# RWKV-5 attention and a multiplicative FFN: the products A on 64x64 array tiles, from a copy of the turned k

## The chip, the core and the metric

The kernel runs on one core of one Trainium2 chip. A core has five engines that run their own instruction queues side by side: TensorE (PE, with its weight loads shown apart as PEld), VectorE (DVE), ScalarE (ACT), GpSimd (POOL) and SyncE (SP), which here only issues DMAs. They hand work to one another by semaphores. The metric is the time of one execution on the device in microseconds (us); lower is better.

## The reference, cut to what matters

```
# r, k, v: (4, 8, 768, 48) = batch, head, token, head_dim;  w, u: (8, 48)
for t in range(S):
    kt, vt, rt = k[:, :, t], v[:, :, t], r[:, :, t]
    cur = einsum('bhd,bhe->bhde', u[None] * kt, vt)
    y[:, :, t] = einsum('bhd,bhde->bhe', rt, state + cur)
    state = w[None, :, :, None] * state + einsum('bhd,bhe->bhde', kt, vt)

x = y.transpose(0, 2, 1, 3).reshape(3072, 384)
h = (x @ w1) * (x @ w2) @ w3          # w1, w2: (384, 1024), w3: (1024, 1024)
out = h @ w_out                        # (1024, 384), fp32
```

All of it is fp32 for the tolerance. The four FFN weights arrive as float64 and are read as pairs of 32-bit words.

## The kernel before, in words

**Units.** The 768 tokens of a batch are cut into six chunks of 128. A unit is one chunk of one batch: 24 units, n = 4c + b. A chunk has two halves of 64 tokens. The state `st[b]` is carried from half to half.

**What attention does for one unit.** `scale` (L308, VectorE) multiplies k and r by powers of w, so that inside a half the decay between two tokens comes out as a product of one factor of k and one of r. Then k and r are needed with the head dimension on the partitions ("turned"). For the first five units `turn` does it with TensorE transposes and ScalarE copies (L339, L341). From unit 5 on (`free = B + 1`) `turn_blocks` transposes 32x32 blocks on VectorE (L349) and writes them to a scratch tensor in DRAM (L351), and `turn_places` reads them back with four DMAs into the tile `tts[n % 2]` (L360), where the rows stand with 32 tokens together: `[128, 4 token blocks, 8, 32]`. The first four of the eight are k of the four head pairs, the last four are r.

`pairs(n)` then makes on TensorE the 64-token sums of k times v (`up`, L382) and the products A = k times r inside each half (L389). Both go to one PSUM tile, `ps_a`. As lhsT the old code takes k in slices of 32 tokens, since a contiguous slice of `tts` has only 32, so each of 4 head pairs x 4 token blocks x 2 heads is one product: 32 products on 64x32 tiles of the array. VectorE adds `up` to the state (L402, L403), ScalarE copies the state to the padded tiles `wide` (L414, in `spread`), and VectorE puts A under a mask into the tile `AT` (L410). `AT` has been filled beforehand with the diagonal, from u*k*r, by eight ScalarE instructions (L324, in `diagonal`).

`output(n)` makes y on TensorE from `wide` and the turned r (L467), then from `v` and `AT` (L477); ScalarE copies the result to `xT` (L482).

**The FFN beside it.** For a chunk of all four batches (512 tokens) `ab` makes both first products (L494 and L499); ScalarE copies the first out of PSUM (L496), VectorE multiplies the second by it (L500). w3 and w_out are folded into one matrix first (`fold`, L294 to L299). The last product is done by Strassen's seven products (L533, L539 to L547). The PSUM pool `psF` that these share has two buffers.

**The order.** The loop over units in each visit writes, in source order: loads for later units, `diagonal(n+1)`, `scale` and `turn_blocks(n+2)`, a share of FFN steps, `output(n)`, `turn_places(n+2)`, `pairs(n+1)`, and another share of FFN steps. The tile framework then orders each engine's queue itself, by source order among what it takes to be ready, and inserts the waits. So the queue of an engine isn't the source order: `diagonal` of a later unit, for one, goes to ScalarE as soon as one of the two `AT` buffers comes free.

fp32 products go through the array in two passes, so the profile shows two weight loads and two matmuls for each product: 24 units x 32 products x 2 = 1536 for L389.

Buffers that matter here: `vnat` (v with 48 columns of zeros behind each head) has `NV = 4` of them, `krin` 3, `tts` 2, `AT` 2.

Of the kernel before, what the change touches and what calls it, by code (L numbers as in the profile page):

```python
# [8 lines left out]
F32 = mybir.dt.float32  # L9
# [12 lines left out]
def kernel(  # L22
# [34 lines left out]
    nc = tc.nc  # L57
    B, H, S, D = r.shape
    P = 128
    C = 128  # L60
    T = C // 2
# [3 lines left out]
    NP = H // 2  # L65
# [10 lines left out]
    Q = 32  # L76
# [4 lines left out]
    def rows(i):  # L81
        return slice(i * PAD, (i + 1) * PAD)
# [13 lines left out]
        nc.gpsimd.tensor_copy(out=same[rows(a)], in_=ident[rows(a), rows(a)])  # L96


    NIN, NV, NS, NRAW = 3, 4, 2, 3
    krin = [const.tile([C, 2, H, D], F32, name=f"krin{i}") for i in range(NIN)]  # L100
    vnat = [const.tile([C, H, PD], F32, name=f"vnat{i}") for i in range(NV)]
    krs = [const.tile([C, 2, H, PAD], F32, name=f"krs{i}") for i in range(NS)]
    tts = [const.tile([P, C // Q, 2 * NP, Q], F32, name=f"tt{i}") for i in range(2)]
# [15 lines left out]
        nc.gpsimd.memset(t[:, :, :, D:PAD], 0.0)  # L119
    for t in wide[1] + wide[0]:  # L120
        nc.gpsimd.memset(t, 0.0)


    units = [(c, b) for c in range(NCH) for b in range(B)]
# [2 lines left out]
    def load(n, which="krv"):  # L127
        if n >= NU:
            return
        c, b = units[n]  # L130
        ts = slice(c * C, (c + 1) * C)
        for nm, src, dst in (("k", k, krin[n % NIN][:, 0]), ("r", r, krin[n % NIN][:, 1]), ("v", v, vnat[n % NV][:, :, :D])):
            if nm in which:
                nc.sync.dma_start(out=dst, in_=src[b, :, ts, :].rearrange("h t d -> t h d"))
# [25 lines left out]
    for i in range(2):  # L160
# [4 lines left out]
                      in_=u.rearrange("h d -> (h d)").rearrange("(o n) -> o n", o=1).to_broadcast([P, DM]))  # L165
# [15 lines left out]
    with tc.tile_pool(name="once", bufs=1) as once, tc.tile_pool(name="psW", bufs=2, space=PSUM) as psW:  # L181
# [12 lines left out]
        for l in range(LEVELS):  # L194
            n = 1 << l
# [6 lines left out]
        for g in range(2):  # L202
            nc.vector.tensor_copy(out=both[:, g, :, T:], in_=both[:, g, :, :T])
            ps = psW.tile([P, NP, C], F32, tag="w", name=f"ps_p{g}")
# [7 lines left out]
    def program(fast):  # L212
        with ExitStack() as arm:
            body(arm, fast)

    def body(arm, fast):
        tab = arm.enter_context(tc.tile_pool(name="tab", bufs=1))
        work = arm.enter_context(tc.tile_pool(name="work", bufs=2))
# [11 lines left out]
        else:  # L230
# [6 lines left out]
            for l in range(LEVELS):  # L237
                n = 1 << l
# [7 lines left out]
            ps = psT.tile([P, NP, C], F32, tag="t", name="ps_pr")  # L246
# [55 lines left out]
        kT, rT, AT, xT = {}, {}, {}, {}  # L302
# [9 lines left out]
        def diagonal(n):  # L312

            kr = krin[n % NIN]
            ruk = work.tile([C, H, D], F32, tag="ruk", bufs=1, name=f"ruk{n}")
            dg = work.tile([C, H], F32, tag="dg", bufs=2, name=f"dg{n}")
            nc.vector.tensor_mul(ruk, kr[:, 0], kr[:, 1])
            nc.vector.tensor_mul(ruk, ruk, ub)
            nc.vector.tensor_reduce(dg, ruk, AX.X, ALU.add)
            AT[n] = work.tile([C, 2, NP, T], F32, tag="AT", bufs=2, name=f"AT{n}")  # L320
            for p in range(NP):
                for i in range(2):
                    h = 2 * p + i
                    nc.scalar.activation(out=AT[n][:, i, p, :], in_=same, func=COPY, scale=dg[:, h:h + 1])  # L324


        def turned(n):
            if fast:
                kT[n], rT[n] = (tts[n % 2][:, :, g * NP:(g + 1) * NP].rearrange("x z p t -> x p z t") for g in range(2))
            else:  # L330
                tt = tts[n % 2].rearrange("x z e t -> x (z e t)").rearrange("x (e t) -> x e t", t=C)
                kT[n], rT[n] = (tt[:, g * NP:(g + 1) * NP] for g in range(2))

        def turn(n):
            turned(n)
            for g, dst, nm in ((0, kT, "kT"), (1, rT, "rT")):
                ps = psT.tile([P, NP, C], F32, tag="t", name=f"ps_{nm}{n}")
                for p in range(NP):
                    nc.tensor.transpose(ps[:, p, :], krs[n % NS][:, g, 2 * p:2 * p + 2, :].rearrange("t h d -> t (h d)"),  # L339
                                        ident)  # L340
                nc.scalar.copy(out=dst[n], in_=ps.rearrange("x p (z t) -> x p z t", t=Q) if fast else ps)  # L341

# [6 lines left out]
            nc.sync.dma_start(out=scratch[n].rearrange("z f m e -> (z f) (m e)"), in_=tr.rearrange("x m e t -> x (m e t)"))  # L351

        def turn_places(n):
            turned(n)
            for i in range(2):
                for m in range(3):
                    lo, hi = (max(i * D, m * Q), min((i + 1) * D, (m + 1) * Q))
                    if lo < hi:
                        x = i * PAD + lo - i * D
                        nc.sync.dma_start(out=tts[n % 2][x:x + hi - lo].rearrange("f z e t -> f z (e t)"),  # L360
                                          in_=scratch[n][:, lo - m * Q:hi - m * Q, m, :].rearrange("z f e -> f z e"))

        def pairs(n):

            c, b = units[n]
            kk = krs[n % NS][:, 0]
            if fast:
                au = psA.tile([C, 2, 512], F32, tag="a", name=f"ps_a{n}")
                ps = au[:, :, :NP * T].rearrange("s i (p t) -> s i p t", p=NP)
            else:  # L370
                for l in range(LEVELS):
                    level(n, l)
                kk = work.tile([C, H, PAD], F32, tag="rl", bufs=1, name=f"kk{n}")
                nc.gpsimd.tensor_mul(kk, krs[n % NS][:, 0], pn[:, 0])
                au = psA.tile([C, 2, 512], F32, tag="a", name=f"ps_u{n}")

            up = au[:, :, NP * T:NP * (T + D)].rearrange("x a (p e) -> x a p e", p=NP)
            last = c == NCH - 1
            for p in range(NP):
                for i in range(2):  # L380
                    for a in range(1 if last else 2):
                        nc.tensor.matmul(up[rows(i), a, p, :], lhsT=kk[rows(a), 2 * p + i, :],  # L382
                                         rhs=vnat[n % NV][rows(a), 2 * p + i, 0:D], start=True, stop=True)
            if fast:
                for p in range(NP):
                    for z in range(C // Q):
                        for i in range(2):
                            a = z * Q // T
                            nc.tensor.matmul(ps[z * Q:(z + 1) * Q, i, p, :], lhsT=kT[n][rows(i), p, z],  # L389
                                             rhs=rT[n][rows(i), p, 2 * a:2 * a + 2], start=True, stop=True)  # L390
            by = wc.to_broadcast([P, NP, D])
            if c:
                spread(0, n)
            for a in range(1 if last else 2):
                if not c and not a:
                    if fast:
                        nc.vector.tensor_mul(st[b], up[:, a], by)
                    else:
                        nc.vector.tensor_copy(out=st[b], in_=up[:, a])
                elif fast:  # L400

                    nc.vector.tensor_add(st[b], up[:, a], st[b])  # L402
                    nc.vector.tensor_mul(st[b], st[b], by)  # L403
                else:
                    nc.vector.tensor_mul(st[b], st[b], by)
                    nc.vector.tensor_add(st[b], up[:, a], st[b])
                if not a:
                    spread(1, n)
            if fast:
                nc.vector.copy_predicated(AT[n], later.bitcast(I32)[:, None, None, :].to_broadcast([C, 2, NP, T]), ps)  # L410

        def spread(a, n):
            for i in range(2):
                nc.scalar.copy(out=wide[a][n % 2][rows(i), :, i * D:(i + 1) * D], in_=st[units[n][1]][rows(i)])  # L414
# [179 lines left out]
        free = B + 1 if fast else NU + 1  # L594
        scale(0)
        diagonal(0)
        turn(0)
        pairs(0)
        asked = 2
        for c in range(NCH):  # L600
            plan = beside[c]
            if not isinstance(plan[0], list):
                cuts = [len(plan) * m // (2 * B) for m in range(2 * B + 1)]
                plan = [plan[cuts[m]:cuts[m + 1]] for m in range(2 * B)]
            for b in range(B):
                n = c * B + b
                while asked <= (n + 3 if n + 3 >= free else n + 2):
                    load(asked)
                    asked += 1
                if n + 1 < min(NU, free):  # L610
                    scale(n + 1)
                if n + 1 < NU:
                    diagonal(n + 1)
                if n + 1 < min(NU, free):
                    turn(n + 1)
                if free <= n + 2 < NU:
                    scale(n + 2)
                    turn_blocks(n + 2)
                for step in plan[2 * b]:
                    step()  # L620
                output(n)
                if free <= n + 2 < NU:
                    turn_places(n + 2)
                if n + 1 < NU:
                    pairs(n + 1)
                for step in plan[2 * b + 1]:
                    step()
# [41 lines left out]
```

## Time and profile before

| | |
|---|---|
| median of 3 runs | 539.51 us (538.28 to 539.96) |
| profiled execution, span | 536.4 us |
| TensorE busy | 502.8 us, 94% |
| VectorE / ScalarE busy | 282.2 us (53%) / 184.1 us (34%) |
| DMA packets, share of 16 engines | 35.1% |
| A products (L389): matmul busy, instructions | 23.3 us, 1536 |
| granted TensorE clock, mean | 0.987 |

The time is that of the whole execution; the profile's span is from the first to the last instruction of the program. A group's line gives the busy time, the mean of one instruction, and after the bar the idle time of its engine just before such instructions with what ended it. "issue" is idle time for which the profile shows no wait. Matmuls overlap, so the busy time of a group of small ones is much less than count times mean.

### The profile page before, as it was taken

The numbers are of one execution on the slowest core, as the hardware profiler recorded it, in microseconds if no ns is written. First come the engines' busy times: TensorE is split into PE (matmuls) and PEld (weight loads), VectorE is DVE, ScalarE is ACT, GpSimd is POOL, SyncE is SP. The second block draws the span as 40 slices with busy tenths as digits, with TensorE's granted clock in tenths as the row PEclk, the third lists the DMA queues.
The fourth block names the chain that finished last, engine by engine and source line by source line (L and its number), as shares of the span: only waits on it lengthen the run. The fifth ranks groups of instructions, "written<-read, shape, count | busy, mean of one in ns | idle before, by whom it ended". The sixth has DMA issues, their size and how long they took to land.

```text
span 536.4 us, 13739 instructions
## 1 busy us (share of the span) xinstructions
PE 502.8 (94%) x5960; PEld 329.6 (61%) x5960; DVE 282.2 (53%) x616; ACT 184.1 (34%) x468; POOL 5.5 (1%) x22
## 2 busy tenths in 40 slices
PE   2777999998999999999999999999999999999997
PEld 2656555544555566559645974487554777954486
DVE  5789897578764664493642464324531215311342
ACT  3787475466553565430123023113033110000100
POOL 4000000000000000000000000000000000000000
PEclk9788999999999999999999999999999999999999
DMA  7978655757665463340131313202011000000001
GB/s 186 226 179 259 202 133 151 204 165 185 177 181 147 135 194 107 76 104 31 45 90 30 104 55 97 60 27 78 31 60 32 2 31 30 31 29 1 0 0 66
DMA packets 96871, 52.82 MB, mean 98 GB/s; under 512 B 77729, under 2 KB 88226, under 8 KB 96802
## 3 DMA queue, kind: packets, MB, share of 16 engines
q1 hardware_dynamic: 96802, 51.86, 35.1%
q8 instruction: 49, 0.80, 0.6%
q14 instruction: 20, 0.16, 0.1%
HBM read 39.65 MB, written 12.19 MB: 97 GB/s over the span
## 4 chain that ended last, share of the span: by engine, by line
PE 86%; ACT 5%; DVE 4%; issue 2%; DMA 2%; SPq 0%; DVEq 0%; ACTq 0%
PE ps_a L494 23%; PE ps_b L499 22%; PE ps_w L298 8%; PE ps_y L467 4%; PE ps_y L477 4%; PE ps_a12b L533 3%; PE ps_s3t L533 3%; PE ps_s4b L533 3%; PE ps_s1t L533 3%; PE ps_a22t L533 3%; PE ps_s2t L533 3%; PE ps_a11b L533 3%; PE ps_a L389 3%; ACT AT L324 2%; PE ps_a L382 1%
## 5 line engine op out<-in xcount | busy, mean ns | idle before, releaser
L494 PE MATMUL ps_a<-xT,w 128*128 128x512 f32 (+1 forms) x300 | 134.2, 582 | 4.2 <-issue 1.8
L499 PE MATMUL ps_b<-xT,w 128*128 128x512 f32 (+1 forms) x300 | 132.5, 577 | 0.2 <-DVE abt L500 0.2
L499 PEld LDWEIGHTS ps_b<-xT,w 128*128 128x128 f32 x300 | 56.6, 190 | 66.1 <-issue 61.2
L500 DVE TENSOR_TENSOR abt<-ps_b,a 128x512 f32<-128x512 f32 (+1 forms) x50 | 33.4, 669 | 115.4 <-PE ps_b L499 110.3
L494 PEld LDWEIGHTS ps_a<-xT,w 128*128 128x128 f32 x300 | 55.1, 190 | 62.9 <-issue 55.8
L496 ACT COPY a<-ps_a 128x512 f32<-128x512 f32 (+1 forms) x50 | 28.4, 567 | 162.9 <-PE ps_a L494 152.6
L324 ACT ACTIVATE AT<-same,dg 128x64 f32<-128x64 f32 x192 | 48.5, 336 | 0.3
L414 ACT COPY wide<-st 64x192 f32<-64x192 f32 x88 | 30.7, 349 | 44.5 <-PE ps_y L467 27.7
L298 PE MATMUL ps_w<-wo,w3T 128*128 128x384 f32 x128 | 43.1, 490 | 1.7 <-ACT w3T L295 1.7
L308 DVE TENSOR_TENSOR krs<-krin,pn_in 128x768 f32<-128x768 f32 x24 | 22.9, 956 | 21.5 <-PE ps_a L382 15.3
L298 PEld LDWEIGHTS ps_w<-wo,w3T 128*128 128x128 f32 x128 | 23.7, 190 | 17.2 <-ACT w3T L295 2.1
L467 PEld LDWEIGHTS ps_y<-tt,wide 128*32 128x32 f32 x1056 | 18.7, 113 | 24.1 <-issue 13.9
L467 PE MATMUL ps_y<-tt,wide 128*32 128x64 f32 x1056 | 26.0, 228 | 5.5 <-ACT wide L414 3.8
L269 ACT ACTIVATE t<-raw,two 128x512 f32<-128x512 uint32 (+2 forms) x32 | 25.3, 799 | 16.8 <-DVE w3n L267 8.0
L389 PE MATMUL ps_a<-tt 64*32 64x64 f32 x1536 | 23.3, 231 | 4.5 <-issue 4.5
L264 ACT ACTIVATE power<-raw 128x512 f32<-128x512 f32 (+2 forms) x32 | 22.3, 703 | 14.6 <-DMA raw<-in_moe_w_dram 11.1
L265 DVE TENSOR_SCALAR power<-power 128x512 f32<-128x512 f32 (+2 forms) x32 | 14.0, 438 | 23.4 <-ACT power L264 23.4
L477 PE MATMUL ps_y<-AT,vnat 64*64 64x64 f32 x1152 | 23.6, 230 | 0.4 <-DVE AT L410 0.4
L539 ACT COPY m<-ps_a11b 128x192 f32<-128x192 f32 x12 | 3.8, 318 | 57.7 <-PE ps_a11b L533 57.7
L477 PEld LDWEIGHTS ps_y<-AT,vnat 64*64 64x64 f32 x1152 | 20.2, 141 | 4.2 <-DVE st L403 1.5
L389 PEld LDWEIGHTS ps_a<-tt 64*32 64x32 f32 x1536 | 18.5, 109 | 6.7 <-issue 5.3
L349 DVE STREAM_TRANSPOSE tr<-krs 128x768 f32<-128x768 f32 x19 | 18.5, 976 | 0.5
(90 smaller groups left out, 566.5 us busy)
## 6 DMA issues: line engine op xcount, KB each, us to landing
raw<-in_moe_w_dram SPq DMA_DIRECT2D x16, 512.0 KB, 4.7
scratch<-tr SPq DMA_DIRECT2D x19, 384.0 KB, 3.2
raw<-in_moe_w_dram SPq DMA_DIRECT2D x8, 768.0 KB, 5.6
tt<-scratch SPq DMA_DIRECT2D x38, 128.0 KB, 2.7
krin<-in_k_dram SPq DMA_DIRECT2D x24, 192.0 KB, 3.8
krin<-in_r_dram SPq DMA_DIRECT2D x24, 192.0 KB, 4.2
vnat<-in_v_dram SPq DMA_DIRECT2D x24, 192.0 KB, 3.7
out_dram<-osb SPq DMA_DIRECT2D x24, 192.0 KB, 1.9
```

The source lines that it names most:

```text
L269: nc.scalar.activation(out=t, in_=lo, func=IDENTITY, bias=two, scale=2.0 ** -51)
L298: nc.tensor.matmul(ps, lhsT=w3T[:, kc, :], rhs=wo[kc], start=(kc == 0), stop=(kc == KF - 1))
L324: nc.scalar.activation(out=AT[n][:, i, p, :], in_=same, func=COPY, scale=dg[:, h:h + 1])
L389: nc.tensor.matmul(ps[z * Q:(z + 1) * Q, i, p, :], lhsT=kT[n][rows(i), p, z], rhs=rT[n][rows(i), p, 2 * a:2 * a + 2], start=True, stop=True)
L414: nc.scalar.copy(out=wide[a][n % 2][rows(i), :, i * D:(i + 1) * D], in_=st[units[n][1]][rows(i)])
L467: nc.tensor.matmul(to(a, q, g), lhsT=wide[a][n % 2][:, p, j * Q:(j + 1) * Q], rhs=rw[:, p, 2 * a:2 * a + 2] if fast else rw[:, p, rows(a)] ...
L477: nc.tensor.matmul(ps[rows(g), a, q, :], lhsT=vv[rows(a), x:x + PAD], rhs=AT[n][rows(a), h % 2, h // 2, :], start=(a not in held and (a, g ...
L494: nc.tensor.matmul(pa[:, :n], lhsT=w1[:, z, q, js], rhs=xT[c][:, q, ts], start=(q == 0), stop=(q == KM - 1))
L496: nc.scalar.copy(out=a[:, :n], in_=pa[:, :n])
L499: nc.tensor.matmul(pb[:, :n], lhsT=w2[:, z, q, js], rhs=xT[c][:, q, ts], start=(q == 0), stop=(q == KM - 1))
L500: nc.vector.tensor_mul(abt[c, j][:, ts], pb[:, :n], a[:, :n])
L533: nc.tensor.matmul(ps, lhsT=made[c, j][a][:, m * C:(m + 1) * C], rhs=made[b][:, j, :], start=(j == 0), stop=(j == KH - 1))
```

## The change

Three things are done.

1. The turned k is given a tile of its own, `kT`, `[128, 4 pairs, 128 tokens]`, one buffer, in which the 128 tokens of a pair stand together. For the first five units `turn` writes it straight from PSUM. From unit 5 on the new `turn_rows(n + 1)` copies it out of `tts` on ScalarE, right behind `diagonal(n + 1)` in the source: 19 copies of 128x512.
2. With 64 tokens together, A is made from 4 pairs x 2 halves x 2 heads = 16 products with a 64x64 lhsT and a 64x64 tile of the array in place of 32 with 64x32. The sums are the same.
3. To make room in SBUF, `vnat` goes from four buffers to three, and v is loaded for unit n + 2 where it was for n + 3. The k half of `tts` is cleared once at the start on GpSimd, since `turn` no longer writes it.

```diff
-    NIN, NV, NS, NRAW = 3, 4, 2, 3
+    NIN, NV, NS, NRAW = 3, 3, 2, 3
...
+    for t in tts:
+        nc.gpsimd.memset(t[:, :, :NP], 0.0)
...
         def turned(n):
+            kT[n] = work.tile([P, NP, C], F32, tag="kT", bufs=1, name=f"kT{n}")
             if fast:
-                kT[n], rT[n] = (tts[n % 2][:, :, g * NP:(g + 1) * NP].rearrange("x z p t -> x p z t") for g in range(2))
+                rT[n] = tts[n % 2][:, :, NP:].rearrange("x z p t -> x p z t")
...
-                nc.scalar.copy(out=dst[n], in_=ps.rearrange("x p (z t) -> x p z t", t=Q) if fast else ps)
+                nc.scalar.copy(out=dst[n], in_=ps.rearrange("x p (z t) -> x p z t", t=Q) if fast and g else ps)
...
+        def turn_rows(n):
+            turned(n)
+            nc.scalar.copy(out=kT[n].rearrange("x p (z t) -> x p z t", t=Q),
+                           in_=tts[n % 2][:, :, :NP].rearrange("x z p t -> x p z t"))
...
                 for p in range(NP):
-                    for z in range(C // Q):
+                    for a in range(2):
                         for i in range(2):
-                            a = z * Q // T
-                            nc.tensor.matmul(ps[z * Q:(z + 1) * Q, i, p, :], lhsT=kT[n][rows(i), p, z],
+                            nc.tensor.matmul(ps[rows(a), i, p, :], lhsT=kT[n][rows(i), p, rows(a)],
                                              rhs=rT[n][rows(i), p, 2 * a:2 * a + 2], start=True, stop=True)
...
-                    load(asked)
+                    load(asked, "kr")
                     asked += 1
+                load(n + 2, "v")
...
                 if n + 1 < NU:
                     diagonal(n + 1)
+                    if n + 1 >= free:
+                        turn_rows(n + 1)
```

More of the change, by code (lines that the diff above doesn't have):

```diff
@@ L327, in turned @@
         def turned(n):
+            kT[n] = work.tile([P, NP, C], F32, tag="kT", bufs=1, name=f"kT{n}")
             if fast:
-                kT[n], rT[n] = (tts[n % 2][:, :, g * NP:(g + 1) * NP].rearrange("x z p t -> x p z t") for g in range(2))
+                rT[n] = tts[n % 2][:, :, NP:].rearrange("x z p t -> x p z t")
             else:
-                tt = tts[n % 2].rearrange("x z e t -> x (z e t)").rearrange("x (e t) -> x e t", t=C)
-                kT[n], rT[n] = (tt[:, g * NP:(g + 1) * NP] for g in range(2))
+                rT[n] = tts[n % 2].rearrange("x z e t -> x (z e t)").rearrange("x (e t) -> x e t", t=C)[:, NP:]
         def turn(n):
@@ L353, in turn_places @@
         def turn_places(n):
-            turned(n)
             for i in range(2):
```

## The prediction, made before the changed kernel was run

> **What bounds the kernel now.** I read the busy table and slices first, then the chain of waits, then the timeline of single visits, because a mean over 24 visits hides which engine sets the pace of each. From the page:
>
> ```profile
> PE   2777999998999999999999999999999999999997
> ACT  3787475466553565430123023113033110000100
> ...
> q8 instruction: 49, 0.80, 0.6%
> ...
> PE 86%; ACT 5%; DVE 4%; issue 2%; DMA 2%; SPq 0%; DVEq 0%; ACTq 0%
> ...
> L477 PE MATMUL ps_y<-AT,vnat 64*64 64x64 f32 x1152 | 23.6, 230 | 0.4 <-DVE AT L410 0.4
> L389 PE MATMUL ps_a<-tt 64*32 64x64 f32 x1536 | 23.3, 231 | 4.5 <-issue 4.5
> ```
>
> From about 60 us on TensorE is the bound: 9 tenths in nearly every slice and 86% of the chain. So time taken out of TensorE's queue counts, unless ScalarE (5% of the chain) is what a visit waits for. The two last lines are the ones to compare: L477 already runs on 64x64 tiles, L389 on 64x32, and L389 has 4.5 us of idle time without a visible wait.
>
> The timeline of an undisturbed visit (weight loads; start and length in us):
>
> ```profile
> 318.91 0.79 PEld L477 LDWEIGHTS ps_y<-AT,vnat 64*64 64x64 f32 x48
> ...
> 319.61 0.56 PEld L382 LDWEIGHTS ps_a<-vnat,krs 64*64 64x64 f32 x32
> ...
> 320.22 0.80 PEld L389 LDWEIGHTS ps_a<-tt 64*32 64x32 f32 x64
> ...
> 321.12 0.30 PEld L494 LDWEIGHTS ps_a<-xT,w 128*128 128x128 f32 x2
> ```
>
> From start to start: 48 passes of L477 take 0.70 us, 14.6 ns each. 32 of L382, on the same tiles, would take 0.47 at this pace, but 0.61 go by before L389: 0.14 are the change of tile size. 64 of L389 with the change to 128x128 behind them take 0.90.
>
> A visit with the idle time in it:
>
> ```profile
> 403.78 0.59 PEld L389 LDWEIGHTS ps_a<-tt 64*32 64x32 f32 x49
> ...
> 405.31 0.18 PEld L389 LDWEIGHTS ps_a<-tt 64*32 64x32 f32 x15 [0.94 <-issue]
> ```
>
> TensorE stops in the middle of independent products. I counted TensorE's instructions through the trace: the five such stops in L389 (112, 267, 292, 334 and 404 us), one of 1.84 us in L494 at 129.7 and one of 0.87 in L467 at 90.3 all stand at place 193 or 194 modulo 256. Queue q8 moved 0.80 MB in 49 packets, 16 KB each: 256 instructions of 64 bytes. So TensorE ran into the end of a block of its own instructions before the next had come.
>
> ScalarE's part, the chain in visit 13 (the visit named by the unit whose A it makes):
>
> ```profile
> 189.95 0.93 PE ps_y L477 x48
> ...
> 190.90 0.48 ACT xT L482
> 191.38 1.92 ACT AT L324 x8
> 193.30 0.48 ACT w3T L295
> ...
> 193.82 2.20 PE ps_w L298 x6
> ```
>
> L389 isn't on it: TensorE is through with it and waits for ScalarE. The chain goes through AT L324 in this way in visits 5, 11, 13 and 14.
>
> **What the Trainium skill says.** The Trainium skill, "TensorEngine Tiling (Array Packing)", Key Properties: a change of tile size drains TensorE, a change of tile doesn't. The trace agrees: the 0.14 us above. "TensorE: Matmul & The Clock Gate", LDWEIGHTS: a weight load's time goes by its columns. L477 and L382 agree in pace at equal columns, though their moving operands have 64 and 48; half as many loads of twice the columns then gain little in loading itself. "Runtime: NRT & Kernel Launch", Instruction fetch mechanics: instructions come in 16 KiB blocks of 256, and crossing a boundary is mostly hidden. The block size agrees; "hidden" doesn't hold in the dense stretches here. "TensorE: Matmul & The Clock Gate", Architectural detail: ScalarE's queue is strictly first in, first out. The trace has ScalarE standing 2.63 us before L264 for a DMA at 189.41, with later work behind it.
>
> **The change, part by part.**
>
> *Products.* 32 passes in place of 64 and one change of tile size less. Before, L382 and L389 took 321.12 - 319.61 = 1.51 us. After: 64 passes of 64x64 at 14.6 ns = 0.93, plus one change at the end, taken as 0.14 to 0.20: 1.07 to 1.13. The gain is 0.4 us a visit. Visit 13 gives the same before, 192.06 - 190.57 = 1.49. Visits in which L389 lies on the chain: 1, 6 to 10, 12, 15 to 23, sixteen. 16 x 0.4 = 6.4 us. In the other eight it lies beside ScalarE, VectorE or a load and is worth nothing. Bounds: 0.3 x 16 = 4.8 and 0.4 x 24 = 9.6.
>
> *Instruction blocks.* A dense stretch (L467, L477, L382, L389) is 384 instructions before and 320 after. TensorE stops if a whole block of 256 lies in it: 128 places out of 256 before, 64 after, plus about 6 for the slower instructions behind. Chances of 0.52 and 0.27 a visit; seven stops of about 1 us before would become about four. Shifting all places by 64 a visit also gives me four, in other visits. That would be 3 us, but where they fall is luck, and one that falls in a visit paced by ScalarE costs nothing either way: I take 2, from -1 to 5.
>
> *The copy.* 19 times 128x512 on ScalarE. Its nearest rows in the tile view and on the page:
>
> ```profile
> L341 ACT COPY tt<-ps_kT x5: 557/561/588, 12.5 to 47.9; 128x512 f32<-128x512 f32 x5
> ```
> ```profile
> L414 ACT COPY wide<-st 64x192 f32<-64x192 f32 x88 | 30.7, 349 | 44.5 <-PE ps_y L467 27.7
> ```
>
> L341 reads PSUM: 0.56 us. L414 goes from SBUF to SBUF as the new copy does, 349 ns for 192 elements; the price in the Trainium skill, "ScalarE: Activation LUTs", What ACT_TABLE_LOAD costs (186 ns and 0.833 ns an element, 346 ns here) agrees, and gives an estimate of 0.61 us for 512. I take 0.6: 11.6 us busy in all, harmless where ScalarE waits for TensorE, as it does for most of the time after 235 us.
>
> Its wait is dearer. It needs the four DMAs of L360, which start only when `output` has read the old `tts`:
>
> ```profile
> 189.98 2.91 SPq L360 DMA_DIRECT2D tt<-scratch  x4
> ```
> ```profile
> DMA to landing us min/median/max: 2.1/3.0/5.7
> ```
>
> In visit 13 the last of the four is issued between 191.3 and 192.9 and lands near 195. If the copy stands in ScalarE's queue right behind AT L324 (free at 193.3), ScalarE stands until 195 and the w3T copies behind it, for which TensorE waits, come 2.4 us late. If the queue is made with the copy behind them, nothing is lost. The same reckoning gives at most 0.6 in visit 5, 1.5 in 7 (the wide copies), 0.5 in 10, 1.1 in 11, 1.6 in 14 and 0.8 in 17 (m L539); elsewhere the next ScalarE work that TensorE needs is a L496, with the 2.6 us of the other product as slack. Sum between 0 and 8.5. The framework puts instructions where it takes them to be ready, so some will stand behind: I take 3.4, two fifths.
>
> *Nothing:* v one unit later goes into the buffer that `output(n - 1)` frees in both versions, and still has about two visits (over 15 us) for a landing of 3.7. kT with one buffer waits for `pairs` of the unit before, which TensorE has always finished by then. The two memsets on GpSimd (5.5 us busy in all) are needed first at unit 5.
>
> Sum: 539.5 - 6.4 - 2 + 3.4 = 534.5 us.
>
> **The rivals.** *More gain:* the copy always stands behind what TensorE needs (0.5 in place of 3.4), and three stops go: 539.5 - 6.4 - 3 + 0.5 = 530.6. For it: ScalarE is 34% busy. Against it: DMAs take 2.1 to 5.7 us, and the queue order is fixed beforehand. *Slower:* ScalarE becomes the bound of a visit; all of the 8.5 us come, and one more stop: 539.5 - 6.4 + 8.5 + 1 = 542.6. For it: in visits 5, 11, 13 and 14 ScalarE is already what TensorE waits for, and ScalarE has waited for DMAs before. Against it: all have to go wrong at once. *No change:* some 6 us of waits against the 6.4, and the stops merely move: 539.5.
>
> **How the numbers follow.** Chances: forecast 0.50, more gain 0.18, no change 0.13, slower 0.19. Below 537.9 (0.3%) are the forecast and the case of more gain: 0.68 faster, 0.13 the same, 0.19 slower. The range reaches from just below the better case to the slower one, 529.5 to 542.5: what is outside is a gain in all 24 visits, or waits of over 8.5 us.
>
> **What would show it.** Right: L389 with 768 matmuls of 64*64; L382's start to the start of what follows L389 near 1.1 us in place of 1.5; fewer than seven stops; a new ScalarE copy of 0.6 us, 19 times, with waits for tt<-scratch of a few us in all. Wrong: L389's passes slower than 14.6 ns, waits for the copy or for w3T and wide behind it of more than 5 us on TensorE, or as many stops as before.

## The result, and the profile after

| | before | after |
|---|---|---|
| median of 4 runs | 539.38 us (538.28 to 539.96) | 525.77 us (524.83 to 526.36) |
| after to before | | 0.9749 [0.9727, 0.977] |
| profiled execution, span | 536.4 us | 522.9 us |
| stops at the end of an instruction block, from visit 5 on | 7, 9.3 us | 2, 1.5 us |
| start of visit 5 | 69.8 us | 66.4 us |

The changed kernel is 13.6 us faster, 2.5%. The forecast was 534.5 and the range began at 529.5, so the gain is 8.7 us larger than forecast. "Visit" is used as in the prediction, and "stop" for TensorE standing still for over 0.5 us at place 193 or 194 modulo 256 of its instruction count. The length of a stop is the time between the starts of the two loads around it, less the 15 ns of a dense stretch. In L494, where the loads stand 0.43 us apart anyway, that is 0.4 us too much: the seven stops of before are 8.9 us without it.

In the code after, a few lines have moved: L382 is now L389, L389 is L395, L467 is L473, L477 is L483, L324 is L326, L295 is L297, L298 is L300, L494 is L500. The new copy of k is L367.

The same parts of the page as were shown of before (slices, instruction queue, chain, the two groups of 64x64 products):

```profile
PE   2697999999999999999999999999999999999996
...
ACT  3897485566655667330223124222243110001000
...
q8 instruction: 43, 0.70, 0.6%
...
PE 85%; DVE 6%; ACT 4%; SPq 2%; issue 2%; DMA 1%; DVEq 0%; ACTq 0%
...
L483 PE MATMUL ps_y<-AT,vnat 64*64 64x64 f32 x1152 | 24.2, 232 | 1.6 <-DVE AT L416 1.6
...
L395 PE MATMUL ps_a<-tt,kT 64*64 64x64 f32 x768 | 18.3, 230 | 0.7 <-issue 0.7
```

TensorE is the bound as before, and ScalarE's share of the chain didn't grow. The A products are 768 on 64x64, and their idle time without a visible wait went from 4.5 to 0.7 us. Six fewer blocks of instructions were fetched (43 in place of 49 packets).

The timeline of visit 18 after (start and length in us, weight loads):

```profile
309.38 0.79 PEld L483 LDWEIGHTS ps_y<-AT,vnat 64*64 64x64 f32 x48
310.08 0.56 PEld L389 LDWEIGHTS ps_a<-vnat,krs 64*64 64x64 f32 x32
310.54 0.58 PEld L395 LDWEIGHTS ps_a<-tt,kT 64*64 64x64 f32 x32
311.20 0.30 PEld L500 LDWEIGHTS ps_a<-xT,w 128*128 128x128 f32 x2
```

From L389 to what follows L395 there are 1.12 us; before, the same stretch of visit 18 took 1.51. L389 takes 0.46 us up to L395, which is 32 passes at 14.6 ns with nothing on top: the change of tile size that cost 0.14 us there is gone. This is what the Trainium skill, "TensorEngine Tiling (Array Packing)", Key Properties, says of a change of tile that keeps the size.

What is left of the stops, in visit 16 after:

```profile
258.54 0.56 PEld L389 LDWEIGHTS ps_a<-vnat,krs 64*64 64x64 f32 x32
259.00 0.54 PEld L395 LDWEIGHTS ps_a<-tt,kT 64*64 64x64 f32 x27
260.39 0.20 PEld L395 LDWEIGHTS ps_a<-tt,kT 64*64 64x64 f32 x5 [0.85 <-issue]
260.66 0.30 PEld L500 LDWEIGHTS ps_a<-xT,w 128*128 128x128 f32 x2
```

TensorE stands for 0.85 us after 27 of 32 independent loads. There is one more in the trace, 0.6 us in L473 at 86.1.

### The profile page after: what moved, and what is told of

The parts are those of the page before. It is cut to its first block, busy times and chain, and to the rows that moved or that the text cites. A ratio compares the mean times of both kernels' runs of the same rounds, so it can differ in the third digit from the quotient of the medians.

```text
span 522.9 us, 12272 instructions
## 1 busy us (share of the span) xinstructions
PE 495.6 (95%) x5192; PEld 324.3 (62%) x5192; DVE 281.8 (54%) x616; ACT 195.7 (37%) x487; POOL 6.0 (1%) x23
## 4 chain that ended last, share of the span: by engine, by line
PE 85%; DVE 6%; ACT 4%; SPq 2%; issue 2%; DMA 1%; DVEq 0%; ACTq 0%
PE ps_b L505 22%; PE ps_a L500 22%; PE ps_w L300 8%; PE ps_y L483 4%; PE ps_y L473 3%; PE ps_s3t L539 3%; PE ps_s4b L539 3%; PE ps_s1t L539 3%; PE ps_a22t L539 3%; PE ps_a12b L539 3%; PE ps_s2t L539 3%; PE ps_a11b L539 3%; PE ps_a L395 2%; PE ps_a L389 1%; ACT AT L326 1%
## 5 line engine op out<-in xcount | busy, mean ns | idle before, releaser
L500 PE MATMUL ps_a<-xT,w 128*128 128x512 f32 (+1 forms) x300 | 134.8, 586 | 0.0
L500 PEld LDWEIGHTS ps_a<-xT,w 128*128 128x128 f32 x300 | 56.1, 192 | 58.4 <-issue 53.0
L326 ACT ACTIVATE AT<-same,dg 128x64 f32<-128x64 f32 x192 | 48.7, 336 | 0.3
L300 PE MATMUL ps_w<-wo,w3T 128*128 128x384 f32 x128 | 43.1, 490 | 2.3 <-ACT w3T L297 2.3
L300 PEld LDWEIGHTS ps_w<-wo,w3T 128*128 128x128 f32 x128 | 23.7, 190 | 17.8 <-ACT w3T L297 2.8
L473 PEld LDWEIGHTS ps_y<-tt,wide 128*32 128x32 f32 x1056 | 18.4, 112 | 23.7 <-issue 15.9
L473 PE MATMUL ps_y<-tt,wide 128*32 128x64 f32 x1056 | 25.3, 226 | 6.3 <-ACT wide L420 3.6
L266 ACT ACTIVATE power<-raw 128x512 f32<-128x512 f32 (+2 forms) x32 | 22.4, 706 | 10.6 <-DMA raw<-in_moe_w_dram 9.7
L483 PE MATMUL ps_y<-AT,vnat 64*64 64x64 f32 x1152 | 24.2, 232 | 1.6 <-DVE AT L416 1.6
L483 PEld LDWEIGHTS ps_y<-AT,vnat 64*64 64x64 f32 x1152 | 20.7, 144 | 6.4 <-DVE AT L416 2.0
L267 DVE TENSOR_SCALAR power<-power 128x512 f32<-128x512 f32 (+2 forms) x32 | 14.0, 439 | 10.8 <-ACT power L266 10.6
L488 ACT COPY xT<-ps_y 128x384 f32<-128x384 f32 x24 | 11.4, 475 | 21.4 <-PE ps_y L483 15.8
L395 PE MATMUL ps_a<-tt,kT 64*64 64x64 f32 x768 | 18.3, 230 | 0.7 <-issue 0.7
```

Source lines behind the costliest of these rows:

```text
L300: nc.tensor.matmul(ps, lhsT=w3T[:, kc, :], rhs=wo[kc], start=(kc == 0), stop=(kc == KF - 1))
L395: nc.tensor.matmul(ps[rows(a), i, p, :], lhsT=kT[n][rows(i), p, rows(a)], rhs=rT[n][rows(i), p, 2 * a:2 * a + 2], start=True, stop=True)
L473: nc.tensor.matmul(to(a, q, g), lhsT=wide[a][n % 2][:, p, j * Q:(j + 1) * Q], rhs=rw[:, p, 2 * a:2 * a + 2] if fast else rw[:, p, rows(a)] ...
L483: nc.tensor.matmul(ps[rows(g), a, q, :], lhsT=vv[rows(a), x:x + PAD], rhs=AT[n][rows(a), h % 2, h // 2, :], start=(a not in held and (a, g ...
L500: nc.tensor.matmul(pa[:, :n], lhsT=w1[:, z, q, js], rhs=xT[c][:, q, ts], start=(q == 0), stop=(q == KM - 1))
```

## The experiments

Two things needed separating: the products (fewer and shorter passes) from the stops, and both from the copy and the later v. The first theory was that the stops follow from the place of each instruction alone, so that any shift of the count changes the time. The rival was that they belong to the 64x32 products, or that the gain comes from the start of the kernel.

**Where the stops fall: shifted copies of both kernels.** Some small products, whose result nobody reads, are put at the head of TensorE's queue. That moves the count of everything behind them and changes nothing else in the queues.

```diff
+        pad = psW.tile([P, T], F32, tag="pad", bufs=1, name="pad")
+        for x in range(26):
+            nc.tensor.matmul(pad[0:Q, :], lhsT=ident[:, 0:Q], rhs=ident[:, 0:T], start=True, stop=True)
```

Four instructions for each: 26 products move the kernel before by 104 places, 44 by 176; 34 and 22 move the changed kernel by 136 and 88.

> The kernel before, with 26 small products ahead of everything (104 more TensorE instructions, done while TensorE waits for its first data). Nothing else in any queue changes; only the ends of the 256-instruction blocks fall elsewhere. Theory (a stop wherever a whole block lies in a dense stretch, less the 32 or so instructions for which the next block is asked ahead): stops leave visits 9, 16, 17, 19 and 22 and come in visits 5, 10, 11, 12, 13, 14, 15, 18 and 23, besides 7; some ten in place of seven, 11 us in place of 7, of which some 2.5 are hidden behind ScalarE in visits 5, 11, 13 and 14: about 541.5 us (540.5 to 543). Rival (the stops belong to certain visits, to DMA traffic or to the 64x32 tiles as such): the same visits as before, 539.4 us.

> The same with 44 small products, 176 instructions. Theory: stops in visits 11, 19, 20 and 21, and a short one in 6; about 5 us in place of 7: 537.5 us (536.5 to 539). Rival: the same visits as before, 539.4 us.

> The changed kernel with 34 small products ahead, 136 instructions. Theory: no stop of over 0.5 us is left; the two of the changed kernel (0.3 and 0.7 us) go: 524.8 us (524.0 to 525.6). Rival: no difference, 525.8 us.

> The changed kernel with 22 small products ahead, 88 instructions. Theory: stops of about 1 us in visits 9, 11 and 17, that of visit 11 partly hidden behind ScalarE: 3 us in place of 1, 527.0 us (526.2 to 528.0). Rival: no difference, 525.8 us.

Measured beside the kernel before (539.64 us): the kernel before shifted by 104, 535.39 us, ratio 0.9918 [0.9894, 0.9942]; by 176, 535.04, 0.9925 [0.9904, 0.9945]. The changed kernel shifted by 136, 524.13, 0.9714 [0.9679, 0.9749]; by 88, 525.92, 0.9751 [0.9715, 0.9786].

So the kernel before gains 0.8% from 104 or 176 instructions that compute nothing. The stops did move. In the kernel before shifted by 104 one now stands in visit 18, which had none:

```profile
314.87 0.61 PEld L481 LDWEIGHTS ps_y<-AT,vnat 64*64 64x64 f32 x35
315.39 0.56 PEld L386 LDWEIGHTS ps_a<-vnat,krs 64*64 64x64 f32 x32
316.01 0.72 PEld L393 LDWEIGHTS ps_a<-tt 64*32 64x32 f32 x59
317.76 0.14 PEld L393 LDWEIGHTS ps_a<-tt 64*32 64x32 f32 x5 [1.03 <-issue]
```

L393 is L389 of before, moved by the added lines. But not every stop that had been foretold came: after the shift by 104 those of visits 5, 11, 15, 18 and 23 did and those of visits 7, 10, 12, 13 and 14 didn't; after the shift by 176 visits 6, 11, 19 and 20 did and 21 didn't, and one came in visit 8 that hadn't been foretold. A block of 256 that lies wholly in a dense stretch isn't enough for a stop. Both shifted kernels before had been expected at a different time, too (541.5 and 537.5), so the rule was incomplete. The changed kernel shifted by 136 came out near the 524.8 of the theory, though one stop of 1.0 us stayed where none had been foretold; shifted by 88 it came out at its rival's 525.8. The count over the traces below mends the rule.

**One part at a time: v alone, and the copy with the old 32 products.** The first has three `vnat` tiles and v loaded for n + 2, nothing else; a twin has the later load with four tiles. The other is the whole change except the products:

```diff
-                    for a in range(2):
+                    for z in range(C // Q):
                         for i in range(2):
-                            nc.tensor.matmul(ps[rows(a), i, p, :], lhsT=kT[n][rows(i), p, rows(a)],
+                            a = z * Q // T
+                            nc.tensor.matmul(ps[z * Q:(z + 1) * Q, i, p, :], lhsT=kT[n][rows(i), p, z * Q:(z + 1) * Q],
```

> The kernel before with the v part alone: three v tiles, v loaded for unit n + 2. Theory (the 3.4 us that the changed kernel is ahead when visit 5 begins come from v standing later in SyncE's queue, so that k, r and the first weights come sooner): 3 us less, 536.4 us (535.4 to 538), unless the stops at block ends fall differently. Rival (those 3.4 us come from the copy kT and the shorter products): 539.4 us.

> The same, v loaded for unit n + 2, but with the four v tiles of before. Theory (the order of the loads does it, not the wait for a free tile): like the v part alone, 536.4 us. Rival (the wait of v for the third tile does it, by holding v back still longer): less or no gain, 538 to 539.4 us.

> The changed kernel, with kT and its copy and the later v, but with the 32 products on 64x32 tiles. Theory (the copy costs nothing, since its place in ScalarE's queue is behind what TensorE needs): the time of the v part alone within 1.5 us, about 536.5. Rival (the copy costs the 3.4 us that I took for it): 539.5 to 540.

Measured, beside 539.4 us before: v alone 536.62, 0.9946 [0.9921, 0.997]; with four tiles 538.55, 1.0003 [0.9985, 1.002]; the copy with 32 products 540.13, 1.0014 [1.0, 1.0029]. The whole gain thus lies in going from 32 to 16 products: without that step, the change is worth nothing.

Two of the three weren't as expected. The later load with four tiles gained nothing, where 536.4 had been expected. The copy with 32 products came out at its rival's number (539.5 to 540, the copy costs what I took for it) and not at 536.5: it is 3.5 us above v alone. In the traces 3.0 of that are stops (9.6 against 6.6 us, last table), but the medians alone would also fit a v that gains 2.8 and a copy that costs 3.5. The copy made twice, below, speaks against that cost.

And the stops of the kernel before are back with the 32 products, this one in visit 17 of the kernel with the copy:

```profile
294.37 0.56 PEld L389 LDWEIGHTS ps_a<-vnat,krs 64*64 64x64 f32 x32
294.99 0.51 PEld L396 LDWEIGHTS ps_a<-tt,kT 64*32 64x32 f32 x43
296.81 0.26 PEld L396 LDWEIGHTS ps_a<-tt,kT 64*32 64x32 f32 x21 [1.31 <-issue]
```

**Is it the 64x32 tile or the number of instructions? Each of the 16 products made twice.** The tile stays 64x64, and TensorE's count of instructions is that of the 32 products.

```diff
-                            nc.tensor.matmul(ps[rows(a), i, p, :], lhsT=kT[n][rows(i), p, rows(a)],
-                                             rhs=rT[n][rows(i), p, 2 * a:2 * a + 2], start=True, stop=True)
+                            for x in range(2):
+                                nc.tensor.matmul(ps[rows(a), i, p, :], lhsT=kT[n][rows(i), p, rows(a)],
+                                                 rhs=rT[n][rows(i), p, 2 * a:2 * a + 2], start=True, stop=True)
```

> The changed kernel with each of the 16 products made twice in a row, which writes the same sums again: as many TensorE instructions as before, on 64x64 tiles. Theory (stops come from the number of instructions that stand closely together): 32 more passes at 14.6 ns in some 15 visits are 7 us, and stops of 4 to 6 us come back: 537.5 us (535.5 to 539.5). Rival (stops came with the small tiles): 532.8 us.

Measured: 547.83 us, 1.0163 [1.0131, 1.0195]. Visits 17 and 20 in its trace:

```profile
301.37 0.43 PEld L396 LDWEIGHTS ps_a<-tt,kT 64*64 64x64 f32 x19
302.64 0.54 PEld L396 LDWEIGHTS ps_a<-tt,kT 64*64 64x64 f32 x21 [0.84 <-issue]
...
370.24 0.56 PEld L389 LDWEIGHTS ps_a<-vnat,krs 64*64 64x64 f32 x16
370.70 1.17 PEld L396 LDWEIGHTS ps_a<-tt,kT 64*64 64x64 f32 x64
371.94 0.30 PEld L501 LDWEIGHTS ps_a<-xT,w 128*128 128x128 f32 x2
```

Visit 17 stops again, now in 64x64 products, and so do 7, 9, 16 and 22: five of the six visits in which the copy with 32 products stops. The stops go with the number of small instructions in a row, not with the tile. The time had been expected 10 us lower; it is 22.1 above the changed kernel. The 64 passes take 371.94 - 370.70 = 1.24 us in place of 0.66 (visit 18 after, 311.20 - 310.54), so 0.58 more in each visit, where 32 passes at 14.6 ns in some 15 visits had been expected. From visit 5 on that is 10.7 us in 19 visits, and 2.7 more of stops (last table). The other 9.1 us come before visit 5; 3.5 of them are one stop in L501 at 38.7 us, and the rest wasn't taken apart. The added passes make a product again on the tile just used. They cost 0.58 / 32 = 18 ns each, where a pass of the changed kernel costs 14.6.

**Fewer stops by choice: shifts picked by the mended rule.** With the rule that the block must begin well inside the dense stretch, 51 added products should leave three stops in the kernel with the copy and 32 products, 50 do much the same for v alone, and 11 take the last stops from the changed kernel. A fourth kernel is that last one with each copy L367 made twice.

> The changed kernel with the 32 products on 64x32 tiles, and 51 small products (204 instructions) ahead, so that by the places seen so far stops remain in visits 9, 16 and 19 alone. Theory (stops are made by where the ends of the blocks fall, nothing else): its stops go from 9.9 us to 3.6: 533.8 us (532.5 to 536). Rival: as without the 204 instructions, 540.1 us.

> The changed kernel with 11 small products (44 instructions) ahead: no stop is left by the places seen so far. Theory: 524.4 us (523.6 to 525.2), the fastest of all. Against the 32 products with three stops (533.8) it is then 9.4 us faster, of which 3.6 are stops and some 6 the products' own passes. Rival: no gain over 525.8 us.

> The v part alone with 50 small products (200 instructions) ahead: stops in the same three visits as with the copy and 204 instructions. Theory (the copy costs nothing): the same time as that run within 1 us, 533.5 us (532 to 535). Rival (the copy costs what the two runs without shift differ by, 3.5 us): 530 us.

> The changed kernel with 44 instructions ahead and each of the 19 copies of the turned k made twice, 11.7 us more work on ScalarE. Theory (ScalarE has room where the copies stand): the time of the run with 44 instructions within 0.6 us, 524.6 us. Rival (the copy is on the path in the visits paced by ScalarE): 2 to 4 us more, 526.5 to 528.5.

Measured, beside 539.86 us before: 539.23, 0.9988 [0.9974, 1.0001]; 525.60, 0.9738 [0.9711, 0.9765]; 538.43, 0.9971 [0.9953, 0.9989]; and with each copy twice 525.43, 0.9735 [0.9711, 0.9758].

With 32 products no shift helped as hoped (533.8 and 533.5 us had been expected): seven and five stops in the whole trace, not three. Some fall where no small product stands any more, just behind the stretch, as in visit 17 of the kernel with the copy, shifted by 204:

```profile
294.83 0.77 PEld L400 LDWEIGHTS ps_a<-tt,kT 64*32 64x32 f32 x64
295.70 0.79 PEld L544 LDWEIGHTS ps_a11b<-w,abt 128*128 128x128 f32 x5
297.34 0.46 PEld L544 LDWEIGHTS ps_a11b<-w,abt 128*128 128x128 f32 x3 [0.86 <-issue]
```

All 64 loads of L400 run through, and TensorE stops some ten instructions behind them, at the block's end. With 16 products the shift by 44 leaves no stop at all; in its page the group of A products has no idle time:

```profile
L399 PE MATMUL ps_a<-tt,kT 64*64 64x64 f32 x768 | 18.8, 237 | 0.0
```

Yet it isn't measurably faster than the changed kernel (524.4 had been expected): 1.5 us of stops are gone, but its visit 5 began at 68.1 us instead of 66.4. That is within what the start of the kernel varies by from trace to trace (last table).

The copy made twice adds 10.6 us of busy time to ScalarE (195.6 to 206.2 in the two pages) and nothing to the time (525.43 against 525.60):

```profile
L372 ACT COPY kT<-tt x38: 601/618/621, 56.7 to 397.3; 128x512 f32<-128x512 f32 x38
```

**All traces side by side.** For each trace: the start of visit 5, the stops from then on, the time from visit 5 to the end, and that time without the stops, in us; the last column is the median of the runs.

| kernel | products | visit 5 begins | stops from then on | visit 5 to the end | without stops | time |
|---|---|---|---|---|---|---|
| before | 32 | 69.8 | 7, 9.3 | 466.6 | 457.3 | 539.4 |
| before, shifted 104 | 32 | 70.3 | 5, 5.8 | 462.4 | 456.6 | 535.4 |
| before, shifted 176 | 32 | 68.6 | 5, 6.2 | 464.5 | 458.2 | 535.0 |
| v alone | 32 | 71.6 | 6, 6.6 | 465.4 | 458.7 | 536.6 |
| v later, four tiles | 32 | 69.7 | 7, 9.3 | 467.0 | 457.6 | 538.6 |
| copy, 32 products | 32 | 71.2 | 6, 9.6 | 467.6 | 458.0 | 540.1 |
| the same, shifted 204 | 32 | 70.8 | 6, 7.0 | 467.3 | 460.3 | 539.2 |
| v alone, shifted 200 | 32 | 69.1 | 4, 6.2 | 468.2 | 462.0 | 538.4 |
| after | 16 | 66.4 | 2, 1.5 | 456.4 | 454.9 | 525.8 |
| after, shifted 44 | 16 | 68.1 | 0 | 454.7 | 454.7 | 525.6 |
| the same, copies twice | 16 | 69.0 | 0 | 454.8 | 454.8 | 525.4 |
| after, shifted 136 | 16 | 66.9 | 1, 1.0 | 454.7 | 453.7 | 524.1 |
| after, shifted 88 | 16 | 67.6 | 2, 2.5 | 456.2 | 453.7 | 525.9 |
| after, products twice | 16, twice | 75.5 | 5, 4.2 | 469.8 | 465.6 | 547.8 |

The 32-product kernels have four to seven stops of 5.8 to 9.6 us together, the 16-product kernels at most two of 2.5, wherever the count is shifted to; with the 16 made twice, five are there again. So it isn't luck that the changed kernel lost them.

## Why the forecast was off, step by step

**What bounds it: right.** TensorE is the bound before and after, and what was taken out of its queue came out of the time.

**Products: 6.4 us forecast, about 6.6 measured, but partly elsewhere.** The gain in a steady visit is as said (1.51 to 1.12 in visit 18, 1.50 to 1.09 in visits 20 and 21). From visit 5 on, without stops, the 16-product kernels take 454.4 us on average (five traces) and the 32-product ones 458.6 (eight), which is 4.2; without the outlier of 462.0 it is 3.7. That is nine or ten visits' worth, where the forecast had fifteen (6.0 us). The rest, 2.9 us, lies before visit 5, where the forecast had one visit (0.4 us). That the two sums agree is luck. There the 32 products with v loaded late reach visit 5 at 70.5 (five traces), the 16 products, with v loaded late too, at 67.6 (five). TensorE's clock is low in that part (0.77 between 14 and 36 us before, 0.84 after), so a pass that is saved there may be a longer one; that wasn't tried by itself.

Visit 13 shows why other visits give nothing. The part of its timeline after that answers to the chain shown of before:

```profile
182.44 0.56 PEld L389 LDWEIGHTS ps_a<-vnat,krs 64*64 64x64 f32 x32
...
183.15 2.02 ACT L326 ACTIVATE AT<-same,dg 128x64 f32<-128x64 f32 x8
...
185.07 1.05 ACT L297 COPY w3T<-ps_w3T 128x512 f32<-128x512 f32 x2
...
185.69 2.23 PEld L300 LDWEIGHTS ps_w<-wo,w3T 128*128 128x128 f32 x8 [0.83 <-ACT w3T L297]
...
188.31 0.61 ACT L367 COPY kT<-tt 128x512 f32<-128x512 f32 x1
```

From L389 to L300 there are 3.25 us, and before they were 193.82 - 190.57 = 3.25 as well. TensorE is through sooner and waits longer for w3T (the weight load 0.83 in place of 0.49 us). Here the saved time comes back as a wait, which isn't a cost of the copy.

**Instruction blocks: the step that failed.** "I take 2, from -1 to 5": 7.8 us were gained (9.3 to 1.5; 7.4 without the ordinary spacing in L494). "Seven stops of about 1 us before would become about four": they became two, and the seven were 1.3 us each. What was right is that the stops are block ends, and that shorter stretches have fewer. What was wrong is the window. I took a stop to come wherever a whole block of 256 lies in the dense stretch, which gives 134 places of 256 before and 70 after. I took ten traces (all but those shifted by 44, 200 and 204) and for each block after 60 us that ends in a dense stretch (or between its groups), with at least 200 of its instructions in it, counted how many dense instructions stand ahead of the block:

```
dense instructions ahead of the block   blocks   stops over 0.5 us
57 or more                              36       36   (0.54 to 1.68 us)
31 to 45                                14        4
0 to 30                                  9        1
none, the stretch begins in the block   45        1
```

The four traces left out, whose shifts were picked by this, give 6 of 6, 0 of 4 and 1 of 9 for the first three rows. So, as a rule, TensorE must also have come some 45 places into the dense stretch before the block begins, or the next block is there in time.

The packets of q8, whose times the traces keep, show why. Counted in order, one packet falls to each block, and by the times of the stops it brings the next one. In visit 9 of before, the block that ends in the stop begins at 110.71 us. The packet starts at 111.37 and has landed at 112.59, and TensorE goes on at 113.83. The window from 111.3 to 112.7 has this packet (one, of 0.02 MB), and that from 112.65 to 113.83 has none:

```profile
q8 instruction: 1, 0.02, 5.5%
```

All 62 stops of the fourteen traces end 1.14 to 1.60 us after such a packet has landed. Of the 78 blocks after 60 us that lie wholly in a dense stretch, 48 end in a stop: their packet starts 0.40 to 1.47 us after the block itself does. For the other 30 it starts at most 0.08 us after the block, and mostly before it. A dense block is run in about 1.9 us, and 0.40 us to the packet's start, 0.9 for the packet and 1.1 from landing to use are already 2.4. With slower instructions ahead of the block, TensorE takes longer over the same number of places, so a request made some places ahead comes early enough. How many places ahead it is made, the runs don't settle.

If the lead is the same for both kernels, the windows are not 134 and 70 but, with 45 taken from both, about 89 and 25. Of seven stops, 7 x 25 / 89 = 2 are left. The change to 16 products takes 64 places off a window of some 90, not off 134, and thus most of the stops. The 45 was found from these same traces, so this explains the two stops and doesn't foretell them.

I also gave only two thirds of even that gain, on the ground that some stops fall where ScalarE sets the pace. The kernel before, shifted by 104 and 176, doesn't bear that out: with 3.5 and 3.1 us less of stops from visit 5 on it was 4.3 and 4.6 us faster. But the copy with 32 products, shifted by 204, was only 0.9 us faster with 2.6 us less of stops. What share of a stop comes out of the time isn't settled by these shifts.

The Trainium skill, "Runtime: NRT & Kernel Launch", Instruction fetch mechanics, gives as the reason why fetching is hidden that instructions are dispatched more slowly than they are fetched. Here 48 passes, 96 instructions, start within 0.70 us, 7.3 ns each or 1.9 us for 256, and that is too fast: the fetch comes 0.5 to 1.7 us late, each time.

**The copy: 3.4 us forecast, no cost found. This step failed too.** The tile view of the changed kernel for L367:

```profile
L367 ACT COPY kT<-tt x19: 601/618/620, 54.8 to 395.7; 128x512 f32<-128x512 f32 x19
its engine sat idle before it (us, times) until:
  DMA tt<-scratch: 0.3, 1
who waited for it (us, times):
  PEld ps_a L395: 0.8, 1
  PEld ps_a L500: 0.7, 3
  PEld ps_a11b L539: 0.2, 1
```

Its length was estimated right: 0.618 us, where the estimate from the price in the Trainium skill, "ScalarE: Activation LUTs", What ACT_TABLE_LOAD costs, had been 0.61. Its wait wasn't. ScalarE stood 0.3 us for tt<-scratch, once, where up to 8.5 were thought possible. In visit 13, the dearest case of the forecast, the queue was made with the copy behind the w3T and wide copies that TensorE needs: it starts at 188.31, when its DMAs had landed. I had "some will stand behind: I take 3.4, two fifths"; what was needed was the other answer, "nothing is lost". The copy made twice, at no cost, shows that there is slack left. And the waits for it by L395 and the weight loads of L500 and L539, 1.7 us in all, are waits of the weight loads; no matmul is in the list.

**v later, one kT buffer, memsets: nothing forecast, not fully settled.** With 32 products visit 5 begins at 69.6 on average with v early (three traces) and at 70.5 with v late (five), 0.9 later, which is inside the spread of each of the two. With four tiles there is no change in the time. The median of v alone is 2.8 us below before, and its trace has 2.7 us less of stops; but the execution in that trace took 538.8 us, no less than the profiled one of before (538.2), so the match proves nothing, and what made the other runs faster isn't shown. Everything but the products together, the copy with 32 products, is worth nothing (540.13 against 539.4).

**The sum by what was measured:** 539.4 - 7.8 (stops) - 3.7 (products from visit 5 on) - 2.9 (products before it) + 0.9 (v) + 0 (copy) = 525.9, where 525.8 was measured. The terms are averages over several traces, so an agreement to 0.1 us is luck. Between the two profiled runs alone the split is 7.8 for the stops, 2.4 from visit 5 on and 3.4 before it. The forecast was off by 8.7, of which 5.8 are the stops (7.8 - 2) and 3.4 the copy's wait; the products (0.2) and v (-0.9) take a little of that back.

**The rivals.** "More gain" went the right way on both terms that failed, and had the sizes too small (530.6): it let three stops go instead of five. "Slower" and "no change" rested on the copy's wait, which didn't come.

**Still open.** Where the start of the kernel gets its spread from: in kernels with the same number of products visit 5 begins up to 3 us apart (66.4 to 69.0 with 16, 68.6 to 71.6 with 32). So how much of the 3.4 us between the two profiled runs is due to the change isn't certain. Differences of 1 us between kernels with 16 products, such as 524.1 and 525.8, can therefore not be given a cause, and no version was found that beats the changed kernel by more than the measurement can tell. Open, too, is why v alone shifted by 200 and the copy shifted by 204 take 2 to 4 us more without their stops than the other kernels with 32 products.

## What to carry to other kernels

When TensorE shows idle time with no wait in the midst of independent small products, count its instructions: if the stops all stand at the same place modulo 256, it is running out of instructions, and the cure is fewer of them in a row, not faster ones. What counts is whether the packet with the next block starts before the block at work does, and so how far a dense stretch exceeds a block plus some lead. A cut of a sixth in the stretch (384 to 320) took most of the stops here. And a new instruction on an engine that is a third busy is priced by where the planned queue puts it: ask whether its data are there at that place before putting down a wait.

## What the runs showed of the hardware that was not expected

- Adding 104 or 176 instructions that compute nothing at the head of TensorE's queue made the kernel before 0.8% faster, by moving the ends of its instruction blocks.
- A block of 256 instructions with 57 or more dense ones ahead of it stopped TensorE every time (36 of 36 in ten traces, 6 of 6 in the other four). The stop ended 1.1 to 1.6 us after the packet with the next block had landed. The stop can come some ten instructions behind the dense stretch, in large products that look innocent.
- The same stop isn't always as long. The one in L494 left the weight loads idle for 2.24 us in the kernel before and 0.57 with v alone (0.24 is ordinary between these loads). The share of the DMA engines in 127 to 133 us (one digit for 0.15 us), first before:

```profile
DMA  9367888788799999999999997311000000099999
...
q8 instruction: 1, 0.02, 1.1%
```

and with v alone:

```profile
DMA  9568866322110000065389830000000025629776
```

Before, TensorE stood from 129.3 to 131.5, and the DMA engines were full up to 130.8; with v alone TensorE stood from 131.8 to 132.4, and they had been idle from 130.6 to 131.8. The packet with the next block started 2.97 us after the block at work in before and 0.79 with v alone, and the DMA engines were 85% and 1% busy in between. This suggests that a block of instructions waits its turn behind data. But with the four v tiles the same packet came after 0.95 us, with the engines 75% busy, so their load alone doesn't settle it; it wasn't tried by itself.
- A 64x64 product made again right behind itself cost 18 ns a pass, against 14.6 for the passes of the changed kernel (1.24 against 0.66 us for 64 and 32 passes).
